# Two PSUM tiles for the weights' words and the third product bank, layer two's first pair in the plain form, and the sums of x spread over seven steps

## The chip, the cores and the metric

The kernel runs on one core of a Trainium2 chip. The metric is the device time of one execution in microseconds: the median of three runs, beside which one execution was profiled.

## What is computed

Three stages, one behind the other, on 1536 tokens of width 512. A retention with a decaying state turns q, k and v into x; then two layers of the same shape follow (512 to 2048 to 512), the first with a Softplus, the second with a scaled square:

```python
h = x @ w_in
g = np.maximum(h, 0.0) + np.log1p(np.exp(-np.abs(h)))
x = g @ w_out
h = x @ w_in2
r = np.maximum(h, 0.0)
g = s * (r * r) + b
y = g @ w_out2
```

The weights arrive as 64-bit numbers, and the result has to be as exact as a float32 computation. So each matrix is carried as two parts, a high and a low one, and a product is three matmuls: high by high, high by low, low by high.

## The kernel before

The tokens are three tiles of 512 (j = 0, 1, 2). A layer's 2048 inner columns are 16 blocks of 128. For one block and one tile, the first product (x by `w_in`, into one PSUM bank) is 12 matmuls of 128x512, and the second (by `w_out`, into four banks `acc`) is 12 more.

**Layer one** goes in 48 steps of a table `steps`, counted from 0: for each of four groups of four blocks, for each tile, four blocks. A step s issues the first product of its block (`h_mm`), and the second product of step s - 2 (`acc_mm`). Between them VectorE and ScalarE make g: `act_0` and `act_2` on VectorE, `act_1` (Softplus) on ScalarE, then the split into `gh` (a copy, ScalarE, `act_hi`) and `gl` (a subtraction, VectorE, `act_lo`). After the fourth block of a group and tile the four `acc` banks are added to `xa[j]` (`take_out`, VectorE); in the last group `xa[j]` is then split into `xh[j]` (ScalarE) and `xl[j]` (GpSimd), the input of layer two.

**The weights** are made on the way. One half of a block (`w_in` or `w_out`) comes by a DMA of 512 KB as pairs of 32-bit words (`raw`, four buffers), and `split_w` builds a float32 word from each pair on VectorE: L282, L286, L291, each into a scratch area x, and L297, which reads x and writes `wm`. ScalarE then copies the high part (`wh`), GpSimd subtracts for the low one (`wl`). From the end of the first stage on, the scratch area x lies in PSUM: it is half of the tile `un` (two banks, pool `ps_s`), in layer two `un[:, 1]`.

**Layer two** goes by pairs of blocks (eight; function `second`, p = 0 to 7). For tiles 0 and 1 and the two blocks of a pair, the first product is done as a 2x2 matrix of quarter products by a scheme with seven products instead of eight, of 6 matmuls each (`six`). It needs sums of quarters of the weights (`sums_w`: four `ws` on GpSimd, then `sh` and `sl`) and sums of quarters of x (`mixed_x`, once). Tile 2 is done plainly, two products of 12 (`all_of`), and the six second products of the pair are 12 each (`acc_2`): 138 matmuls in all. A pair is six parts. The first to the fifth part each start the building of a piece of the next pair's weights, some of its instructions ahead of the part's second product and some behind it, so that VectorE's queue has them between the takes. The products go into three PSUM banks: `one` (pool `ps_h`), `two` (pool `ps_y`), and `three`, which is `un[:, 0]`:

```python
one, two, three = bank(ps_h, "h"), bank(ps_y, "y"), un[:, 0]
```

`three` takes a product of the first part (read by VectorE in `joined`) and the first `all_of` in the fifth part (read by ScalarE in `flat`). Instructions run on each engine in the order in which the code writes them, across engines they wait on semaphores; the waits follow from the tiles that the instructions read and write.

**The join.** In step 45 `mixed_x(1)` makes one sum of x, in step 46 `mixed_x(2)` three more; each is a subtraction of 128x1024 on VectorE, a copy on ScalarE and a subtraction on GpSimd. The last two steps' second products, and the takes of tile 2, lie in the first pair.

Of the kernel before, what the change touches and what calls it, by code (L numbers as in the profile page):

```python
# [13 lines left out]
P = 128  # L14
# [7 lines left out]
TT = 512  # L22
# [25 lines left out]
def tile_retention_mlps(ctx: ExitStack, tc: tile.TileContext, qk, kv, w1, w2, sb, consts, out):  # L48
# [17 lines left out]
    ps_s = ctx.enter_context(tc.tile_pool(name="ps_s", bufs=1, space=bass.MemoryType.PSUM))  # L66
# [197 lines left out]
    w_t, m_t, s_t = {}, {}, {}  # L264

# [6 lines left out]
    def split_w(w, i, pause):  # L272
# [6 lines left out]
        x = (un[:, 1 if w >= NF else i] if spare() else word()).bitcast(U32)  # L279
# [46 lines left out]
    steps = [(la, g, j, f4) for la in range(2) for g in range(NG) for j in range(NTILE) for f4 in range(FG)]  # L326
    h_t, l_t, gg_t, acc_t = {}, {}, {}, {}

    def h_mm(s):
        la, g, j, f4 = steps[s]  # L330
        wh, wl = w_t[la * NF + g * FG + f4, 0]
# [28 lines left out]
    def act_2(s):  # L360
        ps = h_t.pop(s)
        t2 = tp.tile([P, TT], F32, tag="t2", name="t2")
        nc.vector.scalar_tensor_tensor(  # L363
            out=t2, in0=ps, scalar=0.0, in1=l_t[s], op0=ALU.max,
            op1=ALU.add if steps[s][0] == 0 else ALU.mult,
        )
        l_t[s] = t2

    def act_3(s):
        t2 = l_t[s]  # L370
        if steps[s][0] == 1:
            nc.vector.tensor_scalar(
                out=t2, in0=t2, scalar1=sbt[:, 0:1], scalar2=sbt[:, 1:2], op0=ALU.mult, op1=ALU.add
            )
# [12 lines left out]
    def acc_mm(s, banks):  # L387
        la, g, j, f4 = steps[s]
        wh, wl = w_t[la * NF + g * FG + f4, 1]
# [4 lines left out]
        for some in parts:  # L394
            for cc in banks:
# [5 lines left out]
                for i in some:  # L401
                    nc.tensor.matmul(  # L402
                        acc_t[la, g, j][cc], *ops[i], start=f4 == 0 and i == 0, stop=f4 == FG - 1 and i == 2
                    )

    def take_out(s, cc):
# [8 lines left out]
        if g == NG - 1:  # L415
            if j != 1 or cc >= KC // 2:
                split(xh[j][:, cc, :], xl[j][:, cc, :], dst, nc.scalar, nc.gpsimd)


    x_t = []  # L420
    T_AT = 3 * NTILE * FG + 2 * FG + 1

    def mixed_x(part):
# [3 lines left out]
        def one(to, x, y, hi, lo):
            nc.vector.tensor_tensor(out=to, in0=x, in1=y, op=ALU.subtract)
            split(hi, lo, to, nc.scalar, nc.gpsimd)
            x_t.append((hi, lo))  # L430

        def room(name):
            return [late.tile([P, 2, TT], F32R, tag=name + k, name=name + k) for k in "hl"]

        if part == 1:
            one(b11, b12, b11, *room("t1"))
            return
        third = xh[1][:, 0:2], xl[1][:, 0:2]
        one(b12, b22, b12, *third)
        one(b22, b22, b11, *room("t2"))  # L440
        one(b21, b21, b22, *room("t4"))
        x_t[1], x_t[2] = x_t[2], x_t[1]
# [64 lines left out]
    def take_2(p, j, cc):  # L507
        ps, dst = acc_t[1, p, j][cc], xa[j][:, cc, :]
        if p == 0:
            nc.vector.tensor_copy(dst, ps)  # L510
        else:
            nc.vector.tensor_tensor(out=dst, in0=ps, in1=dst, op=ALU.add)  # L512
# [4 lines left out]
    NS = len(steps) // 2  # L517
# [99 lines left out]
    with tc.manual_schedule():  # L617
# [87 lines left out]
        late = ctx.enter_context(tc.tile_pool(name="late", bufs=1))  # L705
        for s in range(SB, NS):
            old = s - LAG
            takes = steps[old][3] == FG - 1
            late_work = work
            work = split_next(s + 1) if not takes and nxt[0][0] < NF + 2 else iter(())  # L710
# [9 lines left out]
            if s == T_AT:  # L720
                mixed_x(1)
# [11 lines left out]
            if s == T_AT + 1:  # L733
                mixed_x(2)
            go(work, 2)

        def second(p):
            w = NF + 2 * p
            first, more = p == 0, p < PAIRS - 1
# [9 lines left out]
            t1, t2, t3, n4 = x_t  # L749
# [5 lines left out]
            one, two, three = bank(ps_h, "h"), bank(ps_y, "y"), un[:, 0]  # L755
# [4 lines left out]
            six(three, a12, b21, True)  # L760
# [155 lines left out]
```

## Time and profile before

| | |
|---|---|
| median of 3 runs | 627.61 us (626.72 to 628.24) |
| profiled execution, its own time | 627.36 us |
| its span, first to last instruction | 625.3 us |
| TensorE matmuls busy | 581.6 us, 93% of the span |
| VectorE, ScalarE, GpSimd busy | 423.6, 318.5, 243.5 us |
| TensorE's mean granted clock | 0.975 |

The span is what the trace covers; the profiled execution's own time has 2.06 us around it. A busy share is a mean over three stages with different limits: the retention fills the first part, layer one runs from about 100 to 320 us, layer two from there on. Waits are told as the engine and line that waited, and the instruction that ended the wait.

### The profile page before, as it was taken

Reading aid. Unit: us, or ns where it says so; the run is one execution under the profiler, and the core shown is the slowest. Engines: PE = TensorE matmul, PEld = TensorE weight load, DVE = VectorE, ACT = ScalarE, POOL = GpSimd, SP = SyncE. Lnnn points to the kernel's source line nnn. Section 1 sums busy time; section 2 is a strip of 40 time slices with the busy share of each in tenths; the row PEclk is TensorE's granted clock in tenths of the full one; section 3 lists DMA queues with packets and bytes.
Section 4 is the critical chain, followed back from the end, with each engine's and each line's share of the span. In section 5 each row is a group of like instructions: output and inputs, shape, how many; then the busy total and the mean of one; then the engine's idle time right before and its main releaser. Section 6 shows DMA issues by size and latency. Waiting matters only on the chain.

```text
span 625.3 us, 7946 instructions
## 1 busy us (share of the span) xinstructions
PE 581.6 (93%) x2980; PEld 473.0 (76%) x2980; DVE 423.6 (68%) x624; ACT 318.5 (51%) x571; POOL 243.5 (39%) x200
## 2 busy tenths in 40 slices
PE   8989999999999999999888897979899797989997
PEld 7777778888888888887666686868678686867875
DVE  4898764979999978987886374656637465563323
ACT  3656563353333324334448756566655756665460
POOL 3557441111111201127457636272642727265040
PEclk9999999999999999999889898989979998998999
DMA  8984112222322211230102221121121112100005
GB/s 332 416 296 154 49 54 68 68 69 67 102 66 68 68 52 50 68 101 5 64 1 67 67 68 56 46 69 39 62 68 65 55 49 68 35 0 1 1 7 194
DMA packets 14869, 50.57 MB, mean 81 GB/s; under 512 B 1776, under 2 KB 1776, under 8 KB 14832
## 3 DMA queue, kind: packets, MB, share of 16 engines
q1 hardware_dynamic: 14832, 50.08, 23.4%
q8 instruction: 23, 0.38, 0.2%
q14 instruction: 14, 0.11, 0.0%
HBM read 46.93 MB, written 3.15 MB: 80 GB/s over the span
## 4 chain that ended last, share of the span: by engine, by line
PE 78%; DVE 11%; ACT 3%; POOL 3%; DMA 2%; issue 2%; SPq 1%; DVEq 0%; POOLq 0%
PE acc L503 20%; PE acc L402 17%; PE h L338 10%; PE y L338 7%; PE h L447 6%; PE s L455 5%; PE y L455 3%; PE y L447 3%; DVE xa L512 2%; PE y L189 2%; PE s L447 2%; DMA kv<-kv 2%; DVE wm L297 1%; POOL xl L114 1%; DVE gl L385 1%
## 5 line engine op out<-in xcount | busy, mean ns | idle before, releaser
L114 POOL TENSOR_TENSOR wl<-wm,wh 128x512 fp32r<-128x512 f32 x64 | 83.7, 1308 | 220.9 <-ACT wh L111 203.3
L512 DVE TENSOR_TENSOR xa<-acc,xa 128x512 f32<-128x512 f32 x84 | 52.4, 684 | 78.6 <-PE acc L503 78.5
L114 POOL TENSOR_TENSOR gl<-c,gh 128x512 fp32r<-128x512 f32 x48 | 61.5, 1288 | 112.1 <-ACT gh L111 98.5
L358 ACT ACTIVATE t<-t 128x512 f32<-128x512 f32 x48 | 30.2, 629 | 95.5 <-DVE t L347 95.4
L402 PE MATMUL acc<-gl,wh 128*128 128x512 f32 x192 | 76.2, 397 | 2.0 <-DVE gl L385 2.0
L402 PE MATMUL acc<-gh,wh 128*128 128x512 f32 x192 | 76.5, 398 | 1.1 <-ACT gh L381 1.1
L503 PE MATMUL acc<-wh,gh 128*128 128x512 f32 x192 | 75.3, 392 | 2.0 <-DVE xa L512 2.0
L503 PE MATMUL acc<-wh,gl 128*128 128x512 f32 x192 | 74.9, 390 | 0.0
L111 ACT ACTIVATE wh<-wm 128x512 fp32r<-128x512 f32 x64 | 39.8, 622 | 51.0 <-DVE wm L297 50.9
L282 DVE TENSOR_SCALAR s<-raw 128x512 uint32<-128x512 uint32 x54 | 37.1, 688 | 36.8 <-ACT c L478 36.3
L402 PE MATMUL acc<-gh,wl 128*128 128x512 f32 x192 | 58.7, 392 | 0.0
L385 DVE TENSOR_TENSOR gl<-t,gh 128x512 fp32r<-128x512 f32 x40 | 54.1, 1352 | 0.2 <-ACT gh L381 0.2
L503 PE MATMUL acc<-wl,gh 128*128 128x512 f32 x192 | 52.0, 389 | 0.0
L289 ACT ACTIVATE wm<-raw 128x512 f32<-128x512 f32 x64 | 42.1, 658 | 9.9 <-POOL wl L114 9.8
L338 PE MATMUL h<-xh,wh 128*128 128x512 f32 x112 | 44.6, 398 | 2.3 <-DVE t L363 1.7
L402 PEld LDWEIGHTS acc<-gl,wh 128*128 128x128 f32 x192 | 36.5, 190 | 11.0 <-DVE gl L385 3.5
L297 DVE SCALAR_TENSOR_TENSOR wm<-wm,s 128x512 f32<-128x512 f32 x54 | 37.2, 688 | 11.3 <-ACT wm L289 5.5
L503 PEld LDWEIGHTS acc<-wh,gh 128*128 128x128 f32 x192 | 36.6, 191 | 10.5 <-issue 1.4
L402 PEld LDWEIGHTS acc<-gh,wh 128*128 128x128 f32 x192 | 36.6, 191 | 9.8 <-ACT gh L381 1.5
L338 PE MATMUL h<-xl,wh 128*128 128x512 f32 x112 | 43.7, 390 | 0.0
L402 PEld LDWEIGHTS acc<-gh,wl 128*128 128x128 f32 x192 | 36.5, 190 | 7.8
L286 DVE SCALAR_TENSOR_TENSOR s<-raw,cu,s 128x512 uint32<-128x512 uint32 x54 | 40.8, 756 | 1.9
(163 smaller groups left out, 1260.7 us busy)
## 6 DMA issues: line engine op xcount, KB each, us to landing
raw<-w SPq DMA_DIRECT2D x64, 512.0 KB, 3.8
qk<-qk SPq DMA_DIRECT2D x12, 512.0 KB, 8.0
kv<-kv SPq DMA_DIRECT2D x12, 512.0 KB, 8.3
out<-xa SPq DMA_DIRECT2D x12, 256.0 KB, 2.1
cst<-consts SPq DMA_DIRECT2D x1, 518.0 KB, 4.1
cst<-consts SPq DMA_DIRECT2D x1, 256.0 KB, 6.5
sbt<-sb SPq DMA_DIRECT2D x1, 1.0 KB, 9.0
```

Of the source, the lines that this page charges most:

```text
L111: nc.scalar.activation(hi, src, AF.Copy)
L114: lo_eng.tensor_tensor(out=lo, in0=src, in1=hi.bitcast(F32), op=ALU.subtract)
L286: nc.vector.scalar_tensor_tensor(out=x, in0=hw, scalar=cu[:, 0:1], in1=x, op0=ALU.bitwise_and, op1=ALU.bitwise_or)
L289: nc.scalar.activation(m, hw.bitcast(F32), AF.Square)
L297: nc.vector.scalar_tensor_tensor(out=m, in0=m, scalar=TINY_SQ, in1=x.bitcast(F32), op0=ALU.is_ge, op1=ALU.mult)
L338: nc.tensor.matmul(ps, w[:, cc * P : (cc + 1) * P], r[j][:, cc, :], start=i == 0, stop=i == len(ops) - 1)
L385: (eng or nc.vector).tensor_tensor(out=gl, in0=l_t.pop(s), in1=gh.bitcast(F32), op=ALU.subtract)
L402: nc.tensor.matmul(acc_t[la, g, j][cc], *ops[i], start=f4 == 0 and i == 0, stop=f4 == FG - 1 and i == 2)
L447: nc.tensor.matmul(ps, w[a][:, k * P : (k + 1) * P], x[b][:, k], start=start and i == 0, stop=i == len(ops) - 1, skip_group_check=True,)
L455: nc.tensor.matmul(ps, w[a][:, k * P : (k + 1) * P], (xh, xl)[b][j][:, k], start=i == 0, stop=i == len(ops) - 1)
L503: nc.tensor.matmul(acc_t[1, p, j][cc], *ops[i], start=half == 0 and i == 0, stop=half == 1 and i == 2)
L512: nc.vector.tensor_tensor(out=dst, in0=ps, in1=dst, op=ALU.add)
```

## The change

Three edits. First, from the end of the first stage on, the pool of `un` is closed and two PSUM tiles of one bank each are opened, `word` and `third`. In layer two the words are built in `word`, and what was `three` is `third`.

```diff
+        ps_2 = ctx.enter_context(tc.tile_pool(name="ps_2", bufs=1, space=bass.MemoryType.PSUM))
+        bank_2 += [bank(ps_2, "word"), bank(ps_2, "third")]
...
-        x = (un[:, 1 if w >= NF else i] if spare() else word()).bitcast(U32)
+        if bank_2:
+            x = bank_2[w < NF and 1 - i].bitcast(U32)
+        else:
+            x = (un[:, i] if spare() else word()).bitcast(U32)
...
-            one, two, three = bank(ps_h, "h"), bank(ps_y, "y"), un[:, 0]
+            one, other, third = bank(ps_h, "h"), bank(ps_y, "y"), bank_2[1]
```

Second, layer two's first pair is done as six more steps of the loop of layer one, two blocks for each tile, in the plain form (24 matmuls a step). Its square and scaling are ScalarE's, `gl` is VectorE's. `second` starts at p = 1. The weights of the pairs from the second on are built from step 48 on, also in steps with takes.

```diff
-    steps = [(la, g, j, f4) for la in range(2) for g in range(NG) for j in range(NTILE) for f4 in range(FG)]
+    steps = [(0, g, j, f4) for g in range(NG) for j in range(NTILE) for f4 in range(FG)]
+    NS_1 = len(steps)
+    steps += [(1, 0, j, f2) for j in range(NTILE) for f2 in range(2)]
...
+        else:
+            nc.scalar.activation(t2, l_t[s], AF.Square)
...
-            nc.vector.tensor_scalar(
-                out=t2, in0=t2, scalar1=sbt[:, 0:1], scalar2=sbt[:, 1:2], op0=ALU.mult, op1=ALU.add
-            )
+            nc.scalar.activation(t2, t2, AF.Identity, scale=sbt[:, 0:1], bias=sbt[:, 1:2])
...
-    NS = len(steps) // 2
+    NS = len(steps)
+    SUMS_AT = {NS_1 - 2: (1, 3), NS_1 - 1: (2,), NS_1: (0,), NS_1 + 4: (4,)}
...
-            work = split_next(s + 1) if not takes and nxt[0][0] < NF + 2 else iter(())
+            work = split_next(s + 1) if s >= NS_1 or not takes else iter(())
...
-        for p in range(PAIRS):
+        for p in range(1, PAIRS):
```

Third, the sums of x are spread: sums 1 and 3 at the end of step 46 (the third in two halves into `p1` and `p5`), 2 at the end of step 47, 0 at the end of step 48, and the split of sum 3 at the end of step 52. GpSimd's part of a sum is now two pieces of 128x512. All four chunks of `xa[1]` are split into `xh[1]` and `xl[1]`, where before the sum took the place of two.

```diff
+        if k == 3:
+            for c, tag in enumerate(("p1", "p5")):
+                t = late.tile([P, TT], F32, tag=tag, name=tag)
+                nc.vector.tensor_tensor(out=t, in0=b22[:, c], in1=b12[:, c], op=ALU.subtract)
+                x3.append(t)
             return
...
+        to, x, y = {1: (b11, b12, b11), 2: (b22, b22, b11), 0: (b21, b21, b22)}[k]
+        hi, lo = (late.tile([P, 2, TT], F32R, tag=f"x{k}{e}", name=f"x{k}{e}") for e in "hl")
+        nc.vector.tensor_tensor(out=to, in0=x, in1=y, op=ALU.subtract)
+        nc.scalar.activation(hi, to, AF.Copy)
+        for c in range(2):
+            nc.gpsimd.tensor_tensor(out=lo[:, c], in0=to[:, c], in1=hi[:, c].bitcast(F32), op=ALU.subtract)
```

The order of the instructions on TensorE at the seam of the fourth and the fifth part of the second call of `second`, before (`s` is the tile `un`, `acc` the banks of the second product; the semaphore of the engine that is waited for stands in brackets):

```order
L503 MATMUL acc_3334<-wh_2797,gl 128x512 [waits Pool_49]
...
L503 MATMUL acc_3334<-wl_2798,gh 128x512 x2
L503 MATMUL acc_3335<-wl_2798,gh 128x512
L503 MATMUL acc_3336<-wl_2798,gh 128x512
L455 MATMUL s<-xh_105,wh_2980 128x512 [waits DVE_49]
L455 MATMUL s<-xl_108,wh_2980 128x512
```

and the same seam now:

```order
L517 MATMUL acc_3642<-wh_3188,gl 128x512 [waits Pool_49]
...
L517 MATMUL acc_3642<-wl_3189,gh 128x512 x2
L517 MATMUL acc_3643<-wl_3189,gh 128x512
L517 MATMUL acc_3644<-wl_3189,gh 128x512
L469 MATMUL third<-xh_105,wh_3241 128x512
L469 MATMUL third<-xl_108,wh_3241 128x512
...
L469 MATMUL third<-xh_105,wl_3242 128x512 x4
L517 MATMUL acc_3737<-wh_3391,gh 128x512 [waits DVE_49]
```

The matmuls stand in the same order; the first of `all_of` no longer waits for VectorE, the product behind it still does, for the takes.

VectorE's queue from step 45 on, before (`xa_110` is `xa[1]`, `t` the steps' g, L428 a sum of x):

```order
L414 TENSOR_TENSOR xa_110<-acc_2714,xa_110 128x512 [waits PE_49]
...
L428 TENSOR_TENSOR xa_109<-xa_110,xa_109 128x1024 [waits DVE_49]
L363 SCALAR_TENSOR_TENSOR t_2858<-h,t_2839 128x512 [waits Activation_49]
L385 TENSOR_TENSOR gl<-t_2811,gh 128x512 [waits Activation_49]
...
L347 TENSOR_SCALAR t_2888<-y 128x512 [waits PE_49]
L363 SCALAR_TENSOR_TENSOR t_2903<-y,t_2888 128x512 [waits Activation_49]
L385 TENSOR_TENSOR gl<-t_2858,gh 128x512 [waits Activation_49]
L428 TENSOR_TENSOR xa_110<-xa_110 128x1024 [waits DVE_49]
L428 TENSOR_TENSOR xa_110<-xa_110,xa_109 128x1024 [waits DVE_49,Pool_49]
L428 TENSOR_TENSOR xa_109<-xa_109,xa_110 128x1024 [waits DVE_49]
L347 TENSOR_SCALAR t_2938<-h 128x512 [waits PE_49]
```

and now from step 46 on (L452 and L441 are sums, the `word` rows build words of the second pair's weights):

```order
L398 TENSOR_TENSOR gl<-t_2863,gh 128x512 [waits Activation_49]
L452 TENSOR_TENSOR xa_109<-xa_110,xa_109 128x1024
L441 TENSOR_TENSOR p_2923<-xa_110 128x512 [waits DVE_49]
...
L360 TENSOR_SCALAR t_2940<-h 128x512 [waits PE_49]
L377 SCALAR_TENSOR_TENSOR t_2952<-h,t_2940 128x512 [waits Activation_49]
L398 TENSOR_TENSOR gl<-t_2908,gh 128x512 [waits Activation_49]
L452 TENSOR_TENSOR xa_110<-xa_110,xa_109 128x1024 [waits DVE_49,Pool_49]
L286 TENSOR_SCALAR word<-raw 128x512 [waits DMAHW7_49]
...
L398 TENSOR_TENSOR gl<-t_2952,gh 128x512 [waits Activation_49]
L452 TENSOR_TENSOR xa_109<-xa_109,xa_110 128x1024
L295 SCALAR_TENSOR_TENSOR word<-raw,cu,word 128x512 [waits DVE_49]
...
L427 TENSOR_TENSOR xa_111<-acc_2897,xa_111 128x512 [waits PE_49]
```

The sum that stood between the takes and the `gl` of step 44 is gone from there, and the three that stood in a row now have a `gl` between each two.

ScalarE's queue at the same place now, steps 47 to 49 (before, the first pair's banks were copied out here):

```order
L453 ACTIVATE x2h<-xa_110 128x1024 [waits DVE_49]
L365 ACTIVATE t_2980<-y 128x512 [waits PE_49,Activation_49]
L293 ACTIVATE wm<-raw 128x512 [waits DMAHW7_49,Pool_49]
L394 ACTIVATE gh<-t_2952 128x512
L381 ACTIVATE t_2997<-t_2980 128x512 [waits Activation_49]
L453 ACTIVATE x0h<-xa_109 128x1024 [waits DVE_49]
L365 ACTIVATE t_3029<-h 128x512 [waits PE_49]
L387 ACTIVATE t_2997<-t_2997,sbt 128x512 [waits Activation_49]
...
L111 ACTIVATE xh_105<-xa_111 128x512 [waits DVE_49] x2
L394 ACTIVATE gh<-t_2997 128x512 [waits Activation_49]
```

The `gh` of step 48 (the last row) stands behind a sum's copy, a Relu and two copies of `xa[2]`, each of which waits for another engine.

## Rows read from the trace of the kernel before

**Rows 1.** The page's chain that ended last: shares of the span by engine

```profile
PE 78%; DVE 11%; ACT 3%; POOL 3%; DMA 2%; issue 2%; SPq 1%; DVEq 0%; POOLq 0%
```

**Rows 2.** Waits of the span: who waited for whom, us, times, longest

```profile
DVE s L282 <- ACT c L478: 36.3, 7, 6.2
...
PE s L455 <- DVE wm L297: 25.7, 7, 4.0
```

**Rows 3.** Stretches: length, busy us (instructions) by engine, granted clock, DMA share, GB/s

```profile
356.60:393.43 36.83, 33.22 (x140) 27.00 (x138) 20.65 (x32) 23.89 (x39) 18.37 (x16) 0.95 0.19 63
...
467.88:503.11 35.23, 31.62 (x140) 25.82 (x138) 20.65 (x32) 22.57 (x37) 17.88 (x15) 1.00 0.18 60
...
576.72:605.28 28.56, 28.56 (x127) 23.65 (x126) 9.18 (x15) 15.26 (x24) 7.73 (x6) 1.00 0.00 1
303.15:356.60 53.45, 43.03 (x163) 33.54 (x162) 34.23 (x40) 33.10 (x52) 35.58 (x25) 0.90 0.13 41
120.00:300.00 180.00, 179.46 (x791) 147.90 (x790) 160.45 (x217) 68.33 (x120) 41.02 (x32) 1.00 0.21 68
```

**Rows 4.** Timeline, TensorE, around one `all_of`: start, us, instruction [idle before]

```profile
411.11 0.39 PE L503 MATMUL acc<-wh,gh 128*128 128x512 f32 x1
...
417.60 0.50 PE L455 MATMUL s<-xh,wh 128*128 128x512 f32 x1 [3.61 <-DVE wm L297]
...
418.99 0.63 PE L455 MATMUL s<-xl,wh 128*128 128x512 f32 x1
419.42 0.63 PE L455 MATMUL s<-xh,wh 128*128 128x512 f32 x1
...
421.98 0.46 PE L503 MATMUL acc<-wh,gh 128*128 128x512 f32 x1
```

**Rows 5.** Timeline, VectorE, in the same gap

```profile
413.57 2.48 DVE L512 TENSOR_TENSOR xa<-acc,xa 128x512 f32<-128x512 f32 x4 [2.99 <-PE acc L503]
...
416.85 0.69 DVE L297 SCALAR_TENSOR_TENSOR wm<-wm,s 128x512 f32<-128x512 f32 x1
```

**Rows 6.** Timeline, TensorE, the idle starts of the join from 303 to 357

```profile
307.13 0.50 PE L402 MATMUL acc<-gh,wh 128*128 128x512 f32 x1 [1.10 <-ACT gh L381]
309.08 0.50 PE L402 MATMUL acc<-gl,wh 128*128 128x512 f32 x1 [1.45 <-DVE gl L385]
...
321.65 0.50 PE L447 MATMUL h<-xh,wh 128*128 128x512 f32 x1 [2.71 <-DVE t L363]
338.32 0.50 PE L447 MATMUL h<-t4h,wh 128*128 128x512 f32 x1 [1.15 <-DVE c L472]
346.71 0.54 PE L455 MATMUL s<-xh,wh 128*128 128x512 f32 x1 [4.01 <-DVE wm L297]
```

**Rows 7.** Timeline, several engines, producers and users near the gap of rows 4

```profile
408.51 0.68 DVE L472 TENSOR_TENSOR c<-h,p 128x512 f32<-128x512 f32 x1
409.75 0.39 PE L447 MATMUL h<-t4h,wh 128*128 128x512 f32 x1
...
418.02 1.29 POOL L114 TENSOR_TENSOR gl<-c,gh 128x512 fp32r<-128x512 f32 x1 [0.26 <-ACT gh L111]
...
427.75 0.39 PE L503 MATMUL acc<-wh,gl 128*128 128x512 f32 x1
```

**Rows 8.** Timeline, several engines, steps 39 to 46 of layer one

```profile
264.12 0.68 DVE L385 TENSOR_TENSOR gl<-t,gh 128x512 fp32r<-128x512 f32 x1
...
283.34 0.50 PE L402 MATMUL acc<-gl,wh 128*128 128x512 f32 x1 [0.33 <-DVE gl L385]
...
302.41 1.28 DVE L414 TENSOR_TENSOR xa<-acc,xa 128x512 f32<-128x512 f32 x2
306.12 2.36 POOL L114 TENSOR_TENSOR t1l<-xa,t1h 128x1024 fp32r<-128x1024 f32 x1 [6.23 <-ACT t1h L111]
306.47 0.61 ACT L381 ACTIVATE gh<-t 128x512 fp32r<-128x512 f32 x1
307.20 1.83 DVE L385 TENSOR_TENSOR gl<-t,gh 128x512 fp32r<-128x512 f32 x1
```

More of the change, by code (lines that the diff above doesn't have):

```diff
@@ L299, in split_w @@
         )
+        m_t[w, i] = m
         if pause:
@@ L402, in acc_mm @@
                     nc.tensor.matmul(
-                        acc_t[la, g, j][cc], *ops[i], start=f4 == 0 and i == 0, stop=f4 == FG - 1 and i == 2
+                        acc_t[la, g, j][cc], *ops[i], start=f4 == 0 and i == 0, stop=ends(s) and i == 2
                     )
@@ L414, in take_out, with mixed_x @@
             nc.vector.tensor_tensor(out=dst, in0=ps, in1=dst, op=ALU.add)
[L415 to L423, printed above, removed]
-        (b11, b21), (b12, b22) = ((xa[j][:, 0:2], xa[j][:, 2:4]) for j in (0, 1))
[L427 to L436, printed above, removed]
-            return
[L438 to L442, printed above, removed]
+        if la == 0 and g == NG - 1:
+            split(xh[j][:, cc, :], xl[j][:, cc, :], dst, nc.scalar, nc.gpsimd)
+    x_t = {}
+    x3 = []
+    def mixed_x(k):
+        (b11, b21), (b12, b22) = ((xa[j][:, 0:2], xa[j][:, 2:4]) for j in (0, 1))
+        if k == 3:
[3 more added lines that the diff above has]
+                x3.append(t)
+            return
+        if k == 4:
+            hi, lo = xh[1][:, 0:2], xl[1][:, 0:2]
+            for c in range(2):
+                split(hi[:, c], lo[:, c], x3[c], nc.scalar, nc.gpsimd)
+            x_t[3] = hi, lo
+            return
+        to, x, y = {1: (b11, b12, b11), 2: (b22, b22, b11), 0: (b21, b21, b22)}[k]
+        hi, lo = (late.tile([P, 2, TT], F32R, tag=f"x{k}{e}", name=f"x{k}{e}") for e in "hl")
+        nc.vector.tensor_tensor(out=to, in0=x, in1=y, op=ALU.subtract)
+        nc.scalar.activation(hi, to, AF.Copy)
+        for c in range(2):
+            nc.gpsimd.tensor_tensor(out=lo[:, c], in0=to[:, c], in1=hi[:, c].bitcast(F32), op=ALU.subtract)
+        x_t[k] = hi, lo
     def six(ps, w, x, start):
@@ L508, in take_2 @@
         ps, dst = acc_t[1, p, j][cc], xa[j][:, cc, :]
[L509 to L512, printed above, removed]
+        nc.vector.tensor_tensor(out=dst, in0=ps, in1=dst, op=ALU.add)
         if p == PAIRS - 1:
@@ L738, in second @@
             w = NF + 2 * p
-            first, more = p == 0, p < PAIRS - 1
+            first, more = p == 1, p < PAIRS - 1
             def part():
@@ L759, in second @@
             p1 = kept(one, "p1")
-            six(three, a12, b21, True)
+            six(third, a12, b21, True)
             if first:
                 act_3(NS - 1)
-            c11 = joined(three, p1)
+            c11 = joined(third, p1)
             go(work, 2)
@@ L774, in second @@
             work = part()
-            six(two, s1, t1, True)
-            p5 = kept(two, "p5")
+            six(other, s1, t1, True)
+            p5 = kept(other, "p5")
             six(one, s2, t2, False)
@@ L792, in second @@
             work = part()
-            six(two, s4, b22, False)
-            c12 = joined(two, u2)
+            six(other, s4, b22, False)
+            c12 = joined(other, u2)
             six(one, s3, t3, False)
@@ L816, in second @@
             work = part()
-            all_of(three, (ah, al), 2)
-            ha = flat(three)
+            all_of(third, (ah, al), 2)
+            ha = flat(third)
             go(work, 2)
@@ L823, in second @@
             go(work, 3)
-            two = bank(ps_y, "y")
-            all_of(two, (bh, bl), 2)
-            hb = flat(two)
+            other = bank(ps_y, "y")
+            all_of(other, (bh, bl), 2)
+            hb = flat(other)
             acc_2(p, 0, 1)
```

35 lines of the change are left out of this document (19 added, 16 removed).

## The prediction

> **What bounds the kernel now.** I read the chain of work that ended last first: 78% of the span is TensorE, 11% VectorE [rows 1]. So what can be had is time in which TensorE stands still or runs slowly. The waits of the whole span say where: TensorE waits seven times, 25.7 us in all, at L455 (`all_of` into `s`, the bank that the code calls `three`) for VectorE's L297 [rows 2]. L297 is the last of the four steps that build the words of a weight. It reads `un[:, 1]`; TensorE writes `un[:, 0]`. They share no word; they share the tile `un`, and the wait is on the tile. The mirror of it is VectorE's 36.3 us at L282 for ScalarE's L478, which reads `un[:, 0]`.
>
> The stretches give the size. In the last pair of blocks no words are built, and 126 matmuls take 28.56 us [rows 3]: 0.2267 us each, with TensorE never idle and the granted clock 1.00. A pair has 138 matmuls (seven products of 6, two of 12, six of 12), so 31.28 us without a gap; the pair at 356.60 takes 36.83 [rows 3]. One such gap close up: the product at 411.11 has 12 matmuls, so the next could start 2.72 us later, at 413.83; it starts at 417.60, after an idle 3.61 us, and it lasts until 421.98, 4.38 us instead of 2.72, since inside it the starts lie 0.43 us apart (418.99, 419.42): the lower clock level, 1.2 GHz, after the idle stretch [rows 4]. That makes 3.77 + 1.66 = 5.43 us in a pair. What TensorE waits for there is plain in VectorE's queue: the four takes of 2.48 us from 413.57, then L291 and L297, which ends at 417.54 [rows 5].
>
> **The two tiles.** `word` and `third` are now a tile each. The order shows the first matmul of `all_of` into `third` without the wait on VectorE. Six pairs from 356.60 to 576.72 take 220.12 us and need 6 x 31.28 = 187.7: 32.4 us go. Is something else late next? Nothing was moved inside a pair, so everything that TensorE waits for behind the gap comes nearer by 5.4 us. Three things hang there. The takes of the third part must be out before the product that follows `all_of`: the four end at 416.05 [rows 5], the product would begin at 413.83 + 2.72 = 416.55 and needs the first two only, so it is covered by more than 0.5 us. `gl` of the fourth bend is written by GpSimd from 418.02 to 419.31 and used at 427.75 [rows 7]; moved up by 5.4 that is 422.3, and 3.0 us are left. Ahead of the gap nothing changes: the second join of the third part ends at 409.19 and the product that overwrites its bank begins at 409.75 [rows 7], 0.56 us of slack, the tightest place of a pair and the same as before, since TensorE ran without a gap up to there already. The other engines have room: in 36.83 us VectorE is busy 20.65, ScalarE 23.89, GpSimd 18.37 [rows 3], all below 31.28.
>
> **The first pair in the old form.** It takes 6 steps of 24 matmuls = 144 instead of 138: 6 x 0.2267 = 1.36 us more. It costs VectorE nothing that matters: Relu, square and scaling of these steps are ScalarE's.
>
> **The join of the layers.** From 303.15 (step 46's first matmul) to 356.60 (second pair) there are 48 + 114 = 162 matmuls, 36.73 us, and it takes 53.45 [rows 3]: 16.7 us are lost, at five starts [rows 6]: 1.10 and 1.45 behind `gh` and `gl`, 2.71 behind L363, 1.15 behind a join, 4.01 at the first `all_of`, and the slow matmuls behind three of these. All this is replaced. A perfect join and perfect pairs give 625.3 - 32.4 - 16.7 + 1.36 = 577.5 us.
>
> The join will not be perfect, because its work is the same and only spread. I walked the queues from 301.8 on, as the order gives them, with 0.60 us for a VectorE step behind another (two takes in 1.28, the last of them 0.68) and 0.61 for ScalarE's [rows 8], 1.29 for a GpSimd piece of 128x512 [rows 7], and a VectorE subtraction held until the GpSimd instruction that runs ends, and 0.55 longer: alone it takes 0.68; beside a GpSimd piece from 306.12 to 308.48 it takes 1.83 and ends at 309.03 [rows 8]. Three places come out late.
> - Step 46: step 45 now takes out j=1 and splits it, as step 41 did for j=0, where TensorE idled 0.33 us [rows 8]. From VectorE's two takes at 302.41 [rows 8] it is two copies, a Softplus and `gh` on ScalarE (to 305.5) and then the `gl` of step 44, held until GpSimd's second piece ends near 306.4: `gl` comes near 306.95. TensorE wants it at 303.15 + 13 x 0.2267 = 306.1: 0.85 us late.
> - Step 50: ahead of `gh` of step 48 ScalarE has `x0h` (behind VectorE's last sum, near 323.5), a Relu, a scaling, a square and two `xh` copies (behind two takes that VectorE reaches at 326.2, after four word steps): `gh` comes near 328.7 and `gl` near 329.5 to 330.7, wanted at 328.75: 0.75 to 2 us, I take 1.3.
> - Step 52: `sh` of the next pair waits on ScalarE for GpSimd's four `ws`, which lie behind four `xl` of j=2; queued behind it are the Relu of step 51 and `gh` of step 50: 0.4 to 1 us, I take 0.8.
>
> Sum 3.0 us. Both ends: 0, if the walk is late by a step everywhere (TensorE's own delay at one place is slack at the next), and 6, if each place is double. No slow clock is charged: the pair at 467.88 has its whole gap and yet a granted clock of 1.00, its 35.23 us are a gap without slow matmuls [rows 3]. The old join, with its longer gaps, has 0.90 [rows 3], so one slow stage of 1.7 us is in the upper end.
>
> **The sum.** 577.5 + 3.0 = 580.5 us of span. The profiled execution took 627.36 for a span of 625.3, 2.06 around it: 582.6. The median of the runs, 627.61, is 0.25 above that one: **582.8 us**, from 579.6 to 587 for this case.
>
> **Rivals.** *Port pile-up at the join.* From step 45 to `gl` of step 48 VectorE has ten subtractions with both inputs in SBUF (five `gl`, five sums), and GpSimd has thirteen pieces beside them. If each of the ten meets a GpSimd piece at its start and is held all of 1.28 us, that is 12.8 us, where the walk has 3.1; of the rest some 2 us vanish in TensorE's slack, so up to 7.7 more, and a slow stage of 1.7: up to 592, 588 in the middle. For it: the walk itself has five of the ten held. Against it: GpSimd's pieces are halves now, and the sums lie at the end of a step where GpSimd is mostly done.
> The Trainium skill (SBUF — State Buffer, "Who interferes with whom") states it as a rule: a VectorE instruction with two SBUF inputs and a GpSimd instruction that reads SBUF exclude each other for a whole instruction, whoever came first. The 1.83 us beside the 0.68 agree with it [rows 8]; taken for all ten it is the rival's 592, taken only where the walk meets it, the forecast.
>
> *A new wait in each pair.* The 0.56 us at the product of the fourth part [rows 7] is used up if VectorE is held once, by 1.83 - 0.68 = 1.15 us [rows 8]: 0.6 us in each of six pairs, 3.6 in all, 586; with the slow stage of 1.66 behind every one, 597. For it: a place with that wait has been seen once, 1.15 us at 338.32 [rows 6]. Against: the queues in front of it are the same as in pairs that show no wait there.
>
> *The change doesn't do what it says.* If the two banks still came out as one for the waits, six pairs keep their 5.4 us: 582.8 + 32.4 = 615. Against it: the order has no wait at that matmul.
>
> *Slower: the clock.* Every gap that goes is also a rest for TensorE. If the chip granted the lower level because of unbroken work, a matmul would cost 0.43 instead of 0.2267 us [rows 4], 0.20 more; it ends above 628.9 once 46 / 0.20 = 230 of the 1110 matmuls of layer two run so. Against it: 180 us of unbroken matmuls at a granted clock of 1.00 [rows 3], and the low stretches lie behind idle ones only.
>
> **How the numbers follow.** Forecast with its join of 0 to 6 us: 0.72. Port pile-up 0.10, a new wait in each pair 0.11, the wait stays 0.04, the clock 0.02, and 0.01 that something eats the gain exactly. The range from 578.8 (the perfect case less the 0.9 by which the fastest run lies under the median) to 591 holds the forecast, most of the pile-up and the lower part of the per-pair wait: 0.72 + 0.06 + 0.04. A difference of 0.2% (1.25 us) is about what a measurement of this kernel can tell from none. Faster 0.97, the same 0.01, slower 0.02.
>
> **What would show it.** Right: TensorE's waits have no row for `third` behind VectorE's last word step; pairs from the second on last 31.3 us each with the granted clock at 1.00; ScalarE's wait for TensorE at L478 into `s`, and VectorE's for ScalarE, are gone or small; between 303 and the first pair in the seven-product form TensorE idles about 3 us in two to four pieces behind `gh` or `gl`. Wrong: a wait of TensorE that comes back in every pair, whatever its releaser, or a granted clock under 1.00 without an idle stretch ahead of it, or a join that loses more than 6 us.

## The result and the profile after

| | before | after |
|---|---|---|
| median | 627.70 us (626.72 to 628.24, 4 runs) | 588.48 us (587.34 to 589.42, 4 runs) |
| ratio | | 0.9376, 95% interval 0.9352 to 0.9400 |
| profiled execution | 627.36 us | 587.71 us |
| its span | 625.3 us | 585.6 us |
| its mean granted clock | 0.975 | 0.999 |

39.2 us are gone, 6.2%. The forecast was 582.8, from 578.8 to 591.0: the time lies in the range, 5.7 us above the forecast and 1.5 us above the 587 at which the forecast's own case ended. Nearly all of the 5.7 us lie in one place, the join of the layers. Of the four executions of after, two (587.34 us, and 587.71, the profiled one) have a mean granted clock of 0.999 and two (589.25 and 589.42 us) one of 0.997, so where medians differ by 1 to 2 us the traces are set beside them.

The stretches of after, with the columns of [rows 3]: the join from step 46's first matmul to the third pair of blocks, the next five pairs, the last pair.

```profile
302.76:380.70 77.94, 72.52 (x307) 56.66 (x306) 58.51 (x79) 53.21 (x89) 49.57 (x40) 1.00 0.20 64
380.70:537.10 156.40, 156.40 (x691) 129.50 (x690) 100.77 (x152) 114.11 (x183) 91.37 (x76) 1.00 0.16 52
537.10:565.66 28.56, 28.56 (x127) 23.65 (x126) 9.18 (x15) 15.28 (x24) 7.75 (x6) 1.00 0.00 1
```

Five pairs take 156.40 us, 31.28 each to the hundredth, without an idle moment of TensorE and at a granted clock of 1.00; in [rows 3] such pairs took 35.23 and 36.83. The last pair is what it was. In the join 306 matmuls at 0.2267 us would be 69.36 us, and it takes 77.94: **8.6 us are lost there**, 5.42 of them as idle time (77.94 - 72.52).

TensorE's waits of the whole span (waiter, line, releaser: us, times, longest) have no row any more that answers to the 25.7 us of [rows 2]:

```profile
PE acc L415 <- DVE gl L398: 2.1, 6, 0.8
PE acc L517 <- DVE xa L523: 2.0, 2, 1.0
...
PE acc L415 <- ACT gh L394: 1.3, 2, 0.7
```

The place of [rows 4] and [rows 5] now, on the timeline of TensorE and VectorE (start, us, instruction, and in brackets the idle time before it with its releaser). `all_of` into `third` begins at 432.38 with no idle time ahead of it, while VectorE still has the four takes and two word steps before it; the last of them ends at 436.1, when `all_of` is over and TensorE is in the next product:

```profile
432.13 2.48 DVE L523 TENSOR_TENSOR xa<-acc,xa 128x512 f32<-128x512 f32 x4 [1.06 <-PE acc L517]
432.38 0.39 PE L469 MATMUL third<-xh,wh 128*128 128x512 f32 x1
...
435.10 0.39 PE L517 MATMUL acc<-wh,gh 128*128 128x512 f32 x1
435.41 0.69 DVE L301 SCALAR_TENSOR_TENSOR wm<-wm,word 128x512 f32<-128x512 f32 x1
```

The idle starts of TensorE in the join, all nine of them, which answer to [rows 6] (behind the first, the matmul that follows it):

```profile
306.64 0.50 PE L415 MATMUL acc<-gl,wh 128*128 128x512 f32 x1 [0.77 <-DVE gl L398]
306.98 0.39 PE L415 MATMUL acc<-gh,wh 128*128 128x512 f32 x1
...
329.13 0.51 PE L415 MATMUL acc<-wh,gl 128*128 128x512 f32 x1 [0.29 <-DVE gl L398]
340.76 0.51 PE L415 MATMUL acc<-wh,gh 128*128 128x512 f32 x1 [0.64 <-ACT gh L394]
341.56 0.50 PE L415 MATMUL acc<-wh,gl 128*128 128x512 f32 x1 [0.29 <-DVE gl L398]
358.77 0.50 PE L415 MATMUL acc<-wh,gh 128*128 128x512 f32 x1 [0.66 <-ACT gh L394]
359.50 0.50 PE L415 MATMUL acc<-wh,gl 128*128 128x512 f32 x1 [0.23 <-DVE gl L398]
365.91 0.50 PE L461 MATMUL h<-x0h,wh 128*128 128x512 f32 x1 [0.79 <-DVE c L486]
376.68 0.50 PE L517 MATMUL acc<-wh,gh 128*128 128x512 f32 x1 [0.91 <-ACT gh L111]
378.03 0.50 PE L517 MATMUL acc<-wh,gl 128*128 128x512 f32 x1 [0.85 <-POOL gl L114]
```

The first four lie in steps 46, 50 and 52, the three places that the prediction names. The other five lie in the first call of `second`, which it did not walk. Taken from start to start, so that the wider pitch of the first matmuls behind a stop counts too, the four cost 1.07, 0.72 and together 1.50 us, 3.3 in all; the remaining 8.6 - 3.3 = 5.3 us are lost in that first call.

What is queued in front of these waits is seen on ScalarE and VectorE, the same timeline, steps 51 to 53:

```profile
337.40 1.06 ACT L111 ACTIVATE sh<-ws 128x1024 fp32r<-128x1024 f32 x1 [3.56 <-POOL ws L320]
338.36 0.58 ACT L365 ACTIVATE t<-h 128x512 f32<-128x512 f32 x1
340.10 0.61 ACT L394 ACTIVATE gh<-t 128x512 fp32r<-128x512 f32 x1
340.74 0.76 DVE L398 TENSOR_TENSOR gl<-t,gh 128x512 fp32r<-128x512 f32 x1 [3.31 <-ACT gh L394]
...
355.14 0.63 ACT L111 ACTIVATE wh<-wm 128x512 fp32r<-128x512 f32 x1 [4.61 <-DVE wm L301]
355.68 0.58 ACT L475 ACTIVATE p<-h 128x512 f32<-128x512 f32 x1
...
358.11 0.61 ACT L394 ACTIVATE gh<-t 128x512 fp32r<-128x512 f32 x1
```

ScalarE stands 3.56 us at `sh`, which needs GpSimd's `ws`; the Relu of step 51, the scaling and the `gh` of step 50 stand behind it, then VectorE's `gl` 3.31 us behind `gh`, and then VectorE's word steps behind `gl`. The `wh` of the last of these words is where ScalarE stands next, for 4.61 us, and `p1` and the `gh` of the last step are behind that. So, by this reading, one late input goes round through three engines; run 6 tests it. ScalarE is busy 53.21 of 77.94 us here: it does not lack time, it stands at the wrong instruction.

### The profile page after: what moved, and what is told of

Same layout as the page of the kernel before. It is cut to its first block, busy times and chain, and to the rows that moved or that the text cites. A ratio compares the mean times of both kernels' runs of the same rounds, so it can differ in the third digit from the quotient of the medians.

```text
span 585.6 us, 7961 instructions
## 1 busy us (share of the span) xinstructions
PE 568.3 (97%) x2986; PEld 463.7 (79%) x2986; DVE 424.8 (73%) x628; ACT 316.0 (54%) x571; POOL 241.4 (41%) x200
## 4 chain that ended last, share of the span: by engine, by line
PE 76%; DVE 11%; ACT 6%; POOL 4%; issue 2%; DMA 1%; SPq 0%; DVEq 0%; POOLq 0%; ACTq 0%
PE acc L415 19%; PE acc L517 19%; PE h L351 10%; PE y L351 8%; PE h L461 6%; PE y L461 3%; PE y L469 3%; PE third L469 3%; PE y L189 2%; DVE gl L398 2%; PE third L461 1%; DMA qk<-qk 1%; POOL xl L114 1%; POOL ws L320 1%; PE s L173 1%
## 5 line engine op out<-in xcount | busy, mean ns | idle before, releaser
L114 POOL TENSOR_TENSOR gl<-c,gh 128x512 fp32r<-128x512 f32 x42 | 54.4, 1296 | 90.4 <-ACT gh L111 67.7
L517 PE MATMUL acc<-wh,gh 128*128 128x512 f32 x168 | 65.7, 391 | 2.9 <-DVE xa L523 2.0
L517 PE MATMUL acc<-wh,gl 128*128 128x512 f32 x168 | 65.5, 390 | 0.9 <-POOL gl L114 0.9
L398 DVE TENSOR_TENSOR gl<-t,gh 128x512 fp32r<-128x512 f32 x46 | 59.5, 1294 | 7.4 <-ACT gh L394 7.4
L351 PE MATMUL h<-xl,wh 128*128 128x512 f32 x124 | 48.4, 390 | 0.0
L293 ACT ACTIVATE wm<-raw 128x512 f32<-128x512 f32 x64 | 42.2, 659 | 9.9 <-POOL wl L114 9.8
L517 PE MATMUL acc<-wl,gh 128*128 128x512 f32 x168 | 45.6, 389 | 0.0
L517 PEld LDWEIGHTS acc<-wh,gh 128*128 128x128 f32 x168 | 31.5, 188 | 10.5 <-issue 1.4
L517 PEld LDWEIGHTS acc<-wh,gl 128*128 128x128 f32 x168 | 31.5, 188 | 7.7 <-POOL gl L114 1.2
L517 PEld LDWEIGHTS acc<-wl,gh 128*128 128x128 f32 x168 | 31.5, 188 | 6.6
L301 DVE SCALAR_TENSOR_TENSOR wm<-wm,word 128x512 f32<-128x512 f32 x44 | 30.3, 688 | 8.9 <-ACT wm L293 4.2
```

What stands on the lines that cost most here:

```text
L114: lo_eng.tensor_tensor(out=lo, in0=src, in1=hi.bitcast(F32), op=ALU.subtract)
L293: nc.scalar.activation(m, hw.bitcast(F32), AF.Square)
L301: nc.vector.scalar_tensor_tensor(out=m, in0=m, scalar=TINY_SQ, in1=x.bitcast(F32), op0=ALU.is_ge, op1=ALU.mult)
L351: nc.tensor.matmul(ps, w[:, cc * P : (cc + 1) * P], r[j][:, cc, :], start=i == 0, stop=i == len(ops) - 1)
L398: (eng or nc.vector).tensor_tensor(out=gl, in0=l_t.pop(s), in1=gh.bitcast(F32), op=ALU.subtract)
L517: nc.tensor.matmul(acc_t[1, p, j][cc], *ops[i], start=half == 0 and i == 0, stop=half == 1 and i == 2)
```

## The experiments

**1. The tiles alone.** Before, with nothing but the two tiles.

```diff
-    ps_s = ctx.enter_context(tc.tile_pool(name="ps_s", bufs=1, ...))
+    ps_s = ret.enter_context(tc.tile_pool(name="ps_s", bufs=1, ...))
...
-        x = (un[:, 1 if w >= NF else i] if spare() else word()).bitcast(U32)
+        if bank_2:
+            x = bank_2[w < NF and 1 - i].bitcast(U32)
+        else:
+            x = (un[:, i] if spare() else word()).bitcast(U32)
...
+        ps_2 = ctx.enter_context(tc.tile_pool(name="ps_2", bufs=1, ...))
+        bank_2 += [bank(ps_2, "word"), bank(ps_2, "third")]
...
-            one, two, three = bank(ps_h, "h"), bank(ps_y, "y"), un[:, 0]
+            one, two, three = bank(ps_h, "h"), bank(ps_y, "y"), bank_2[1]
```

> The kernel before with one edit: the words in a tile of their own, the third bank in another. Theory (the shared tile is the stall): the seven waits of TensorE at the first all_of vanish, six pairs last 31.3 us each instead of 36.7, 32.4 us go, and the first call of `second` loses its 4.01 us of idle and 1.7 of slow matmuls but gets 2 to 3 us back as waits on the fourth part's g, since that product is one product nearer there: 592 us, 589.5 if nothing is late behind the gap. Rival (the plain first pair and the spread sums bring much of the gain): above 600.

Measured: 590.13 us, ratio 0.9395 (0.9371 to 0.9420). The seven waits at `all_of` are gone. The old join keeps the first four of its five starts, and a smaller wait stands in the place of the fifth:

```profile
307.03 0.50 PE L406 MATMUL acc<-gh,wh 128*128 128x512 f32 x1 [1.13 <-ACT gh L385]
308.98 0.50 PE L406 MATMUL acc<-gl,wh 128*128 128x512 f32 x1 [1.45 <-DVE gl L389]
321.52 0.50 PE L451 MATMUL h<-xh,wh 128*128 128x512 f32 x1 [2.68 <-DVE t L367]
336.56 0.50 PE L451 MATMUL h<-t4h,wh 128*128 128x512 f32 x1 [1.15 <-DVE c L476]
348.18 0.49 PE L507 MATMUL acc<-wh,gl 128*128 128x512 f32 x1 [1.43 <-POOL gl L114]
```

Against the runs of before beside it (628.06) the tiles alone bring 37.9 us, where all three edits bring 39.2. The other two edits together are worth 590.13 - 588.48 = 1.65 us by the medians, 1.4 by the spans (587.0 and 585.6): little more than what a measurement of this kernel can tell from none. The intervals of the two ratios overlap (0.9371 to 0.9420, and 0.9352 to 0.9400), so that the other two edits gain anything is not shown. The theory's 592 counted 2 to 3 us on the fourth part's g, which is one wait of 1.43 us here.

**2. The old dependence alone.** After, with `word` and `third` as the halves of one tile again, and everything else as it is.

```diff
-        bank_2 += [bank(ps_2, "word"), bank(ps_2, "third")]
+        both = ps_2.tile([P, 2, 512], F32, tag="both", name="both")
+        bank_2 += [both[:, 0], both[:, 1]]
```

> The changed kernel with words and third bank as two halves of one tile again. Theory: TensorE waits at the first all_of of every call that builds words, six times, with slow matmuls behind: 5.4 us each, 588.5 + 32.6 = 621, the join unchanged. Rival (in the new arrangement the words' last step comes early enough, since pieces of the weights are one part ahead): under 605.

Measured: 623.92 us (618.52 to 624.80; the profile is of the shortest), ratio 0.9938 (0.9913 to 0.9963), 35.4 us above after. The waits of [rows 2] are back, in both directions, and one that was not foreseen, in the first call of `second`, where L461 writes `third`:

```profile
PE both L469 <- DVE wm L301: 21.2, 6, 3.6
PE both L461 <- DVE wm L301: 4.0, 1, 4.0
...
DVE both L286 <- ACT c L492: 23.6, 5, 5.3
```

No word is shared and no instruction is changed: it is the tile that makes the wait. Runs 1 and 2 together settle the first step of the prediction.

**3. Without the piece in step 53.** After, with the next weights' piece in step 53 left to the parts.

```diff
-            work = split_next(s + 1) if s >= NS_1 or not takes else iter(())
+            work = split_next(s + 1) if (s >= NS_1 or not takes) and s < NS - 1 else iter(())
```

> The changed kernel without a piece of the next weights in step 53; every later piece is built one part later. Theory (ScalarE's queue is held at its head: by wh behind VectorE's L301 ahead of the first call, then by sh behind GpSimd's ws between the joins and their Relu): the waits at step 53's second product (1.45 us lost) and at the last second product of the first call (2.4 us) go, 584.7. Rival (ScalarE and GpSimd have too much work there, wherever it stands): 588 to 589.

Measured: 584.25 us, ratio 0.9306 (0.9282 to 0.9330). The waits of 358.77, 359.50, 376.68 and 378.03 are gone; the second join's grows from 0.79 to 1.15 us:

```profile
364.66 0.50 PE L461 MATMUL h<-x0h,wh 128*128 128x512 f32 x1 [1.15 <-DVE c L486]
...
351.37 0.60 ACT L475 ACTIVATE p<-h 128x512 f32<-128x512 f32 x1 [1.13 <-PE h L461]
```

With `wh` out of the way, `p1` leaves at 351.37 instead of 355.68. The medians differ by 4.2 us; in the traces the 306 matmuls of the join take 74.56 us (302.90 to 377.46) instead of 77.94, and all of the difference lies in the first call. So 3.4 us of the 5.3 lost there are put down to the piece that runs one part ahead of its place.

**4. The second products of the fourth part to the fifth.** After, with the first pair's product moved behind `all_of`.

```diff
-            if first:
-                acc_2(p, 0, 0)
-            else:
+            if not first:
                 acc_2(p - 1, 2, 1)
                 take(2)
...
-            if not first:
-                acc_2(p, 0, 0)
+            acc_2(p, 0, 0)
```

> The changed kernel with the second product of tile 0 and the first block, in the first call of `second`, in the fifth part as in all other calls, not in the fourth. Theory (the fourth part's g is used one product too early in the first call alone): the two waits of 0.91 and 0.85 us there go, 2.4 us with the starts: 586.1. Rival (ScalarE is behind by more than a product): the waits stay, at the same product, 588.5.

Measured: 588.89 us (587.47 to 589.30), nothing against after (the join takes 77.93 us for 77.94), and the same two waits at the same place, the second now 0.86 us at 377.98:

```profile
376.62 0.50 PE L517 MATMUL acc<-wh,gh 128*128 128x512 f32 x1 [0.92 <-ACT gh L111]
```

That is the number of the rival, but the run decides less than it should: between the product of the fourth part and the late one there are as many matmuls with the edit as without it, in another order. It was a poorly chosen edit.

**5. The sums in one step.** After, with the sums of x bunched in step 46 again.

```diff
-    SUMS_AT = {NS_1 - 2: (1, 3), NS_1 - 1: (2,), NS_1: (0,), NS_1 + 4: (4,)}
+    SUMS_AT = {NS_1 - 2: (1, 3, 2, 0), NS_1 + 4: (4,)}
```

> The changed kernel with all four sums of x in a row at the end of step 46 (the split of the third stays at step 52). Theory (the order of the queues decides, the sums' own time is hidden): VectorE comes 2.4 us later to step 47's first instruction, the g of step 46 comes 1 to 2 us too late for TensorE, and step 50's 0.7 us goes, since the last sum's copy no longer stands ahead of it: 588.5 to 590. Rival (spreading the sums is what shortened the join): 593 or more, with idle starts behind g of over 2 us and slow matmuls.

Measured: 592.56 us (591.20 to 592.76), 4.1 above after by the medians, near the rival's 593. VectorE's third and fourth sum take 4.47 us, where each takes 1.21 or 1.22 in after; GpSimd's two pieces of the sums lie against them and take 3.53 us, 1.3 each in after; TensorE stands 2.54 us, and starts lie 0.43 us apart behind it, the lower clock level:

```profile
313.20 3.53 POOL L455 TENSOR_TENSOR x1l<-xa,x1h 128x512 fp32r<-128x512 f32 x2 [2.85 <-ACT x1h L453]
313.33 4.47 DVE L452 TENSOR_TENSOR xa<-xa,xa 128x1024 f32<-128x1024 f32 x2
...
319.99 0.50 PE L415 MATMUL acc<-gh,wh 128*128 128x512 f32 x1 [2.54 <-ACT gh L394]
...
321.38 0.63 PE L415 MATMUL acc<-gh,wh 128*128 128x512 f32 x1
...
321.81 0.63 PE L415 MATMUL acc<-gl,wh 128*128 128x512 f32 x1
...
381.53 0.50 PE L517 MATMUL acc<-wh,gl 128*128 128x512 f32 x1 [0.86 <-POOL gl L114]
...
382.44 0.63 PE L517 MATMUL acc<-wh,gh 128*128 128x512 f32 x1
```

In after, one of the same sums and a `gl` that does meet a GpSimd piece:

```profile
316.37 1.21 DVE L452 TENSOR_TENSOR xa<-xa,xa 128x1024 f32<-128x1024 f32 x1
...
320.27 1.58 DVE L398 TENSOR_TENSOR gl<-t,gh 128x512 fp32r<-128x512 f32 x1 [1.29 <-ACT gh L394]
```

My theory for this run fell. Two sums without company are 2.4 us; here they are held for another 2.0, and `x0h`, a Softplus and `gh` stand behind them. Matmul by matmul the traces say more than the medians: beside after, 5.0 us are lost in steps 47 and 48, 1.3 come back at steps 50 (0.7, as the theory had it) and 52, and 1.5 more are lost in the first call, where the two stops of after at 376.68 and 378.03 stand again (0.92 and 0.86 us) and are followed here by the lower clock level. So the sums' order is worth some 3.6 us in the trace and 4.1 by the medians, more than the two edits have together (1.65): an estimate from runs 1 and 5 is that the plain first pair with the sums in a row would be some 2.4 us slower than run 1.

**6. `sh` two stops later.** After, with the copy of the sums of weights further back in ScalarE's queue.

```diff
         lo = late.tile([P, 4, KH], F32R, tag="sl", name="sl", bufs=2)
         yield
+        yield
+        yield
         split(hi, lo, t, nc.scalar, nc.gpsimd)
```

> The changed kernel with the high copy of the weights' sums (sh) two places later in the code: in the join behind the next step's g, in the pairs still at the end of its part. Theory (ScalarE's queue held by sh behind GpSimd's ws is what TensorE waits for at step 52): the idle 0.64 and 0.29 us there go, 1.5 us with the starts, 587.0; the waits in the first call of `second` stay. Rival (GpSimd's subtractions hold VectorE's gl): the 0.29 stays and 588.

Measured: 583.33 us, ratio 0.9284 (0.9264 to 0.9304), a gain of 5.1 us by the medians, and of 4.1 in the join of the traces (73.87 us, 302.92 to 376.79), where 1.5 were expected. The four idle starts from 340.76 to 359.50 are gone, not only the two behind `sh`, and the one of step 46 falls from 0.77 to 0.33. ScalarE no longer idles ahead of `sh`. It waits 1.43 us for the same `ws` at L293, still ahead of the `gh` of step 50, which comes 2.4 us earlier than in after all the same; and it stands a shorter time at the `wh` of step 53:

```profile
306.35 0.50 PE L417 MATMUL acc<-gl,wh 128*128 128x512 f32 x1 [0.33 <-DVE gl L400]
...
337.12 0.67 ACT L293 ACTIVATE wm<-raw 128x512 f32<-128x512 f32 x1 [1.43 <-POOL ws L320]
337.69 0.61 ACT L396 ACTIVATE gh<-t 128x512 fp32r<-128x512 f32 x1
...
338.73 1.05 ACT L111 ACTIVATE sh<-ws 128x1024 fp32r<-128x1024 f32 x1
...
351.25 0.63 ACT L111 ACTIVATE wh<-wm 128x512 fp32r<-128x512 f32 x1 [2.53 <-DVE wm L301]
```

In after these were 3.56 and 4.61 us of idle time. The second was in good part a child of the first, as read in the queue above: moving one copy of 1.06 us that nobody needs yet takes the first away and nearly halves the second.

**7. The split of x behind `gl`.** After, with the copies of the first two taken chunks (`split_x`) called behind `act_lo`.

```diff
-                take_out(old, 0)
-                take_out(old, 1)
+                take_out(old, 0, True)
+                take_out(old, 1, True)
...
             if s > SB:
                 act_lo(s - 1)
+            if takes:
+                split_x(old, 0)
+                split_x(old, 1)
```

> The changed kernel with the split of the first two taken chunks of x behind g of the step, not ahead of it (steps 41, 45 and 49). Theory (two ScalarE copies and two GpSimd pieces ahead of g make it late): the idle 0.33, 0.77 and 0.29 us at steps 42, 46 and 50 go, 2 us with the starts: 586.4. Rival (step 50 is late because of the sum's copy x0h, step 46 because VectorE comes late to the takes): under half of that, 587.5 to 588.5.

Measured: 587.83 us (587.22 to 588.41). The idle starts of steps 42, 46 and 50 are gone, 2.1 us with the starts, as the theory had it. Of that, 1.2 us are given back at once, at a stop of step 44 that grows from 0.22 to 0.74 us and a new one of 0.30 in step 48. At step 52 TensorE comes 0.8 us earlier than in after, and `gh` 0.4 us later: GpSimd begins the four pieces of `xl` ahead of `ws` at 329.39 instead of 327.23, so `ws`, and with it `sh`, is later than before. TensorE stands 1.87 us instead of 0.64, and starts behind it lie 0.43 us apart for a while:

```profile
294.37 0.50 PE L415 MATMUL acc<-gl,wh 128*128 128x512 f32 x1 [0.74 <-DVE gl L398]
...
337.84 1.06 ACT L111 ACTIVATE sh<-ws 128x1024 fp32r<-128x1024 f32 x1 [4.80 <-POOL ws L320]
...
341.20 0.52 PE L415 MATMUL acc<-wh,gh 128*128 128x512 f32 x1 [1.87 <-ACT gh L394]
```

Step 52 loses 2.6 us against after, and the first call gets 2.1 of them back: its idle starts at 358.77 and 359.50 are gone. The sum is near nothing (77.58 us for the join instead of 77.94), the rival's number but not the rival's reason: the steps that the theory named gained what it said, and steps 44 and 48 and the late `sh` took it.

**8. All of it.** After with the edits of 3, 6 and 7, and the second products of the first call of `second` one part later each (the edit of 9, below).

> The changed kernel with four shifts of order together: no piece of the weights in step 53, sh later, the split of x behind g, and in the first call of `second` the second products of steps 52 and 53 and of tile 0 one part later each, so that a product lies between the second join and the product that overwrites its bank. Theory (all of the 8.6 us that the join loses are heads of queues): what is left of them is under 1.5 us, 580 to 581.5. Rival (the engines lack time in the join): 583 or more, with new waits there.

Measured: 578.67 us (578.58 to 578.85), ratio 0.9213 (0.9195 to 0.9231). The join, with the same 306 matmuls, and all of TensorE's waits in it:

```profile
301.60:371.95 70.35, 69.87 (x307) 57.28 (x306) 54.66 (x75) 51.80 (x87) 49.76 (x40) 1.00 0.20 61
```

```profile
354.13 0.50 PE L468 MATMUL y<-xh,sh 128*128 128x512 f32 x1 [0.48 <-ACT p L482]
```

70.35 - 69.36 = 1.0 us is lost instead of 8.6, as the theory had it. The time is 1.3 us under the theory's 580, also since two idle starts of layer one, in steps 42 and 44, are gone too: the join begins at 301.60 instead of 302.76. The busy times of VectorE, ScalarE and GpSimd in that stretch (54.66, 51.80, 49.76) are nearly what they were (58.51, 53.21, 49.57), in 70.35 us instead of 77.94. No engine was too slow for the join; the order in the queues was.

**9. The shift alone.** After, with the first call's second products one part later and nothing else.

```diff
                 act_hi(NS - 1)
                 act_lo(NS - 1)
-                acc_mm(NS - 2, FIRST + SECOND)
...
             if first:
-                acc_mm(NS - 1, FIRST)
-                ...
+                acc_mm(NS - 2, FIRST + SECOND)
...
-            if not first:
+            if first:
+                acc_mm(NS - 1, FIRST)
+                ...
+            else:
                 acc_2(p - 1, 2, 0)
```

> The changed kernel with only the last of the four shifts: in the first call of `second` the second products of steps 52 and 53 and of tile 0 one part later. Theory (the first call's waits hang on one late queue, ScalarE's): the idle starts at step 53's product and at the fourth part's product go, but the last second product of the call waits for the same g as before, so TensorE stands there longer by what it saved: 588 to 589, with the two waits there at 3 us or more together. Rival (the waits are separate and add up): 586.

Measured: 587.43 us (587.37 to 588.76): 1 us at most against after, within the spread of either, and 77.93 us for the join, as in after. The wait was given back, but not at the place I expected. The product into `h` now comes before `p1` has left that bank, since `p1` still stands behind the `wh` of step 53; the starts behind it lie 0.43 us apart:

```profile
357.51 0.58 PE L461 MATMUL h<-x2h,sh 128*128 128x512 f32 x1 [2.43 <-ACT p L475]
...
360.02 0.63 PE L415 MATMUL acc<-wh,gh 128*128 128x512 f32 x1
360.45 0.63 PE L415 MATMUL acc<-wh,gl 128*128 128x512 f32 x1
```

**10. Without unused sums.** The kernel of 8, without the sums of the first pair's weights, which the plain first pair reads nowhere.

```diff
-        halves += [(w, 0), (w + 1, 0), (w, 2), (w, 1), (w + 1, 1)]
+        halves += [(w, 0), (w + 1, 0)] + [(w, 2)] * (w > NF) + [(w, 1), (w + 1, 1)]
```

> The version with four shifts of order, without the sums of the first pair's weights, which the plain form doesn't use (four ws, sh and sl near 286 us). Theory (TensorE bounds it, all of that is hidden): the same, 578 to 579. Rival (that work still makes some g late): the idle 0.48 us in the first call and up to 1 us go, 577.5.

Measured: 578.16 us (578.01 to 578.50), before in the same runs 626.6, ratio 0.9220 (0.9194 to 0.9245). By its median it is 0.5 us under run 8, by its ratio no better (0.9220 and 0.9213): the two are the same within what a measurement here can tell. Both beat after by some 10 us (588.48 - 578.16 = 10.3).

## Why the prediction was right, and 5.7 us short

- **The bound and the two tiles: right.** Run 1 has 37.9 us by the tiles alone, run 2 puts 35.4 back. Per pair the forecast was 31.28 us and no new wait; after has 31.28. The slacks counted behind the gap held: of the three, none has become a wait in five pairs. The rival of a new wait in each pair falls with that, and so does the clock rival: 184.96 us of unbroken matmuls (156.40 + 28.56) at a granted clock of 1.00. The other waits that were to go, ScalarE's behind the first `all_of` and VectorE's 36.3 us, have no row in after either.
- **The change does what it says: right.** 615 us was the price of the wait staying; from the measured 588.48 that is 588.48 + 32.4 = 620.9, and run 2, which makes the wait stay and has the unforeseen one of 4.0 us besides, measures 623.92.
- **The plain first pair: right in its count**, six matmuls more. What I did not ask is what it moves: its pieces of the next weights run in steps 48 to 53, one part ahead of where `second` expects them.
- **The join came out on the prediction's own sign of being wrong.** It named "a join that loses more than 6 us", and 8.6 are lost. The case that it called its forecast ended at 587; that 588.48 still lies in the stated range is owed to the room up to 591 made for the port pile-up and for a new wait in each pair, and neither came as it was described. That part of the hit is luck. (Its own terms add up to 579.8 and 587.5 where it has 579.6 and 587, and to 596.4 where the per-pair rival has 597; nothing hangs on that.)
- **The join's walk: its three places were right, and their sum was close** (0.85, 1.3 and 0.8 us forecast; 1.07, 0.72 and 1.50 measured; 2.95 against 3.3). The cause named for step 52, the `sh` behind GpSimd's `ws`, is what run 6 showed, though I took its harm for local: its shadow reaches to the `gl` of the last step.
- **The step that failed** is the sentence "Sum 3.0 us. Both ends: 0 ... and 6". The walk ended at step 52 and I gave the first call of `second`, 114 matmuls behind it, a loss of nothing. It loses 5.3 us: `p1` and the last step's `gh` behind the `wh` of step 53, a join, and a `gh` and `gl` of the fourth part that TensorE now reaches with one second product fewer in between than in a full pair. In the old kernel the same stretch showed the waits of [rows 6] at 338.32 and 346.71, and I removed them on paper without walking what would come late instead. The mechanism was the one named, the order in front of ScalarE; its extent was not. That makes 8.6 - 3.0 = 5.6 us; layer one arrived 0.4 us earlier (302.76 for 303.15), so the span is 585.6 where 580.5 was forecast, and the median lies 0.77 above the profiled execution, not 0.25; the forecast charged a slow stage (1.7 us) at its upper end only.
- **The port pile-up** came near the measured time for another reason than its own. From `gl` of step 44 to that of step 48 the five take 1.36, 1.29, 1.10, 1.58 and 0.77 us, held 2.7 us together against 0.68 each, and the sums take 1.21 or 1.22 us and are not held: 2.7 where the walk had 3.1 and the rival 12.8. Run 5 shows when it would have been true: with the sums in a row, two of them need 4.47 us. The rule of the Trainium skill (SBUF — State Buffer, "Who interferes with whom") agrees with run 5's rows: the two sums take 4.47 us there and GpSimd's pieces beside them 3.53, instead of 2.4 and 2.6; whether it costs anything is decided by where the instructions stand.

What stays open: the plain pair without the spreading was not run on the kernel of run 1, so its price is the estimate given with run 5; and why run 6 also shortens the idle start of step 46 was read only from its position (the unused sums of the first pair's weights, which use the same code, move too).

## What to carry to other kernels

Two PSUM banks that share no data still wait for each other as long as they are one tile: where a wait names an instruction whose data the waiter doesn't read, look at the tile first. When a stall is taken away, walk the queues until the steady state is reached and not until the edit ends, and look in each in-order queue for an instruction that waits for another engine and that nobody needs yet; moving it back a few places cost nothing here and gave 4.1 us in the trace, 5.1 by the medians. Fixes around such a head of queue were waited away again here (runs 7 and 9), so remove the head first, or all together (run 8).

## What the runs showed of the hardware that was not expected

- A short stop costs more than its idle time. The nine idle starts of the join have 5.42 us of idle and 8.6 us lost from start to start, so some 0.35 us each on top (3.2 / 9). Of that, 0.16 is that the matmul ahead of a stop counts as busy for its 0.39 us, where in a row the next one starts after 0.23; 0.11 is that the first matmul behind the stop takes 0.50 us and the next starts 0.34 us later instead of 0.23 (306.64, 306.98); the rest lies in the few starts after that, some of them 0.24 or 0.25 us apart. The granted clock is 1.00 throughout.
- Stops much shorter than the 3.61 us of [rows 4] can be followed by the lower clock level too. Behind the idle 2.54 us of run 5 and the 2.43 us of run 9 starts lie 0.43 us apart for a while; behind the 1.87 us of run 7 the granted clock of the next 2.8 us is 0.56. The length of the stop alone does not decide it: behind the 2.68 us of run 1, at 321.52, the starts stay 0.23 us apart (granted clock 1.00), and behind the last two of the nine stops of after, 0.91 and 0.85 us, the clock stays at 1.00, where behind the same two in run 5, 0.92 and 0.86 us, it falls (0.58 from 381.53 to 385.30).
